# A fused delta-rule attention and mixture-of-experts kernel: the prologue's loads one place earlier, chunk 10's scores in the prologue, ten filler products instead of two

## The chip, the cores and the metric

One core of one Trainium2 chip runs the whole program. The metric is device time in microseconds (us) of one execution; a kernel's time is the median of its runs. The profile is of one further execution of the same program, and all times of single instructions are of that execution, counted from the start of its span.

## What is computed

The first half is a recurrence over 768 steps for 4 batches and 8 heads of width 48; its output, one row of 384 numbers per batch and step, goes through a two-level router into one of 16 experts.

```python
def _attn_ref(q, k, v, beta):
    k_n = k / (np.linalg.norm(k, axis=-1, keepdims=True) + 1e-06)
    state = np.zeros((B, H, D, D))
    for t in range(S):
        kt, vt, bt = (k_n[:, :, t], v[:, :, t], beta[:, :, t, None])
        y[:, :, t] = np.einsum('bhd,bhde->bhe', q[:, :, t], state)
        v_old = np.einsum('bhde,bhd->bhe', state, kt)
        state = state + bt[:, :, :, None] * np.einsum('bhd,bhe->bhde', kt, vt - v_old)
    return y

def _moe_ref(x, w_group, w_expert, w1, w2):
    ...
            h = np.maximum(xg[mask_e] @ w1[g, e], 0.0)
            ye = h @ w2[g, e]
            combined = g_w[mask_g][mask_e] * e_w[mask_e]
            out[tok_idx] = combined[:, None] * ye
```

The recurrence gives x of 3072 rows by 384; w1 is 384 by 1024 and w2 1024 by 384 for each expert. All data is 32-bit float.

## The kernel before

**Attention.** The 768 steps are cut into 24 chunks of 32 (NCH = 24), and four chunks make a group (RG = 4). A tile's 128 partitions are 4 batches by 32 steps. For each chunk `gram(u)` (L258 or L273) multiplies the keys with keys and queries on TensorE into PSUM, 32 products that the trace shows as 64 rows; ScalarE copies the two halves out, to `gt` (L278) and `gq` (L284). For each group `inverse(g)` works on VectorE for some 28 us in the prologue: a transpose (L313), a long row of multiply and add pairs (L382, L388), a transpose back into `mt` (L416). ScalarE spreads `mt` into `mtb` (L427), and VectorE makes one part of it (L425). `scale(u)` on VectorE (L463) multiplies the values of a chunk, which come with the tile `kv`, into `vh`.

`advance(u)` is one period of the recurrence, and each step in it needs the one before: products `a_ps` with the state (L486), ScalarE's copy `f` (L490), products `o_ps` with the state (L495), products `w_ps` with the inverse (L503), the copy `w` (L507), products into the state `s_ps` (L514), two copies to `s_bd` (L520), products that end `o_ps` (L528), the copy `x` (L537). Period 0 has no state yet, so it begins with `w_ps`. In each period stands one `gram` too, that of chunk u + LEAD (LEAD = 10), between `w_ps` and `s_ps`, and the three transposes `t_ps` (L554) and routing products `l_ps` (L456) of the chunk before.

**Loads.** Keys and queries of a chunk are one tile `kqt` of 448 KB, in a ring of NB = LEAD + 2 = 12 buffers; values are `kv`, 416 KB, in a ring of three; the constants come in two parts, of which the second (376.5 KB) holds the identity. All these loads are issued by SyncE's queue (SP) in program order.

**What sets the order in the prologue.** The order on every engine is the order of the code. Before period 0 there are twelve half or whole `gram` calls (chunks 0 to 3 keys only, 4 to 7 whole, then the query halves of 0 to 3), and behind them `gram(8)` and `gram(9)`. They write in turn to three places in PSUM, `g`, `begin0` and `begin1`; the last two lie where the state `s_ps` will lie, so the first writer of `s_ps` waits for ScalarE's copies out of them. A load is held back by `begin` (L800): ScalarE writes one column of the tile that the load will fill, and the load waits for that write. `bursts` says behind which `gram` ScalarE does so, and `after_gram` says it for `gram(8)` and `gram(9)`. Because ScalarE works in order, a load's gate opens when the copies of that `gram` are through. Behind `gram(9)` stand two products of the identity with constants (L834), 128 x 128 by 128 x 384, into `s_ps`; nothing reads their result, and the first product of the state overwrites it. Then `w_ps` of period 0 waits for `mtb`.

**Experts.** After the recurrence the rows are sorted by expert, and 16 experts follow one another on TensorE (L1113 and L1132). The change leaves this part alone.

Of the kernel before, what the change touches and what calls it, by code (L numbers as in the profile page):

```python
# [16 lines left out]
C = 32  # L17
RG = 4
SHARE = 0.61
LEAD = 10  # L20
FIXED, TILE = 1, 128
SLOTS = [224] * FIXED + [232, 220, 214, 208, 204, 202, 200, 198, 194, 190, 186, 184, 180, 174, 168]
ACT_STEP, PE_STEP, SOON, NEXT, TURN = "ScalarE", "TensorE", "end of the period", "next period", "its turn"
# [43 lines left out]
def deltanet_then_moe(  # L67
# [13 lines left out]
    nc = tc.nc  # L81
    B, H, S, D = shape
    NP = H // 2
    NCH = S // C
# [28 lines left out]
    wr = cp.tile([128, DC, NL], F32, name="wr")  # L113
# [64 lines left out]
    with ExitStack() as first:  # L178
# [10 lines left out]
        for n in range(2):  # L189
            homes.append(pse.tile([128, 2, 512], F32, tag=f"begin{n}", name=f"begin{n}"))  # L190
        NB, NV = LEAD + 2, 3
        LATE, SMALL, KR = NCH - LEAD, NGR - 1, 64 + D
        ENDING = NCH - 2
        halved = range(LATE, SMALL * RG)
        kqt_ = [ap_.tile([128, 2, NP, 128], F32, name=f"kqt{i}") for i in range(NB)]
        kv_ = [ap_.tile([128, NP * KR + H * D], F32, name=f"kv{i}") for i in range(NV)]

        def load_kq(u, a=None):
            half = slice(0, 2) if a is None else slice(a, a + 1)
            nc.sync.dma_start(out=kqt_[u % NB][0:KR, half],  # L200
                              in_=kq_d[u].rearrange("p (a j t) -> p a j t", a=2, j=NP)[:, half])

        def load_kv(u):
            nc.sync.dma_start(out=kv_[u % NV], in_=kv_d[u])
# [3 lines left out]
        def load_con(i):  # L208
            part = slice(cols[i], cols[i + 1])
            nc.sync.dma_start(out=con[:, part], in_=const_d[:, part])  # L210
# [13 lines left out]
        def of_kq(u, a=None):  # L224
            return (kqt_[u % NB][:, a or 0, 0], [lambda: load_kq(u, a)])

        bursts = {
            1: [of_kq(RG), of_kq(RG + 1)],
            RG: [of_kq(RG + 2), of_kq(RG + 3)],
            RG + 2: [of_kq(u, 1) for u in range(RG)]  # L230
                    + [(wr[:, 0], [lambda: nc.sync.dma_start(out=wr, in_=wr_d)])],
            2 * RG: [(kv_[0], [lambda: load_kv(0), lambda: load_con(1), lambda: load_kv(1)])],
            2 * RG + 2: [of_kq(2 * RG), of_kq(2 * RG + 1)],
        }
        after_gram = {2 * RG: [of_kq(2 * RG + 2), (kv_[2], [lambda: load_kv(2)])],
                      2 * RG + 1: [of_kq(2 * RG + 3), of_kq(NB)]}
        rooted = sm.tile([128, 1], F32, tag="rooted", name="rooted", bufs=1)
        gts, raws, gqs, mts, norm, vhs, xs, turned_over = {}, {}, {}, {}, {}, {}, {}, set()
        begun_with = {}
# [1 line left out]
        def gram(u, home=None, parts=(0, 1), paired=False):  # L241
# [39 lines left out]
            if 1 not in parts:  # L281
                return None
            raws[u] = wk.tile([128, H, C], F32, tag="gq", name=f"gq{u}", bufs=LEAD + 1)
            nc.scalar.activation(raws[u], g_out[:, :, 1, :], ACT.Copy)  # L284
# [471 lines left out]
        def start(task, share):  # L756
            behind.append(task)
            rate[task], due[task] = share, 0.0
# [24 lines left out]
        def allow(what):  # L783

            for task in list(behind):
                if held.get(task) is what:
                    push(task)
# [5 lines left out]
        with tc.manual_schedule(engines={mybir.EngineType.PE, mybir.EngineType.DVE,  # L793
# [3 lines left out]
            def begin(burst):  # L797

                for late, loads in burst:
                    nc.scalar.activation(late[:, 0:1], cut["tiny"], ACT.Copy)  # L800
                    for load in loads:
                        load()
# [19 lines left out]
                                  .to_broadcast([128, 4, 4, BL]))  # L822
            ahead = advance(0)
            next(ahead)
            for u in range(2 * RG, LEAD):
                gram(u, homes[u % len(homes)])
                begin(after_gram[u])
            begin_with.close()
# [1 line left out]
            s_ps = pst.tile([128, B, 512], F32, tag="state", name="s_ps")  # L830
            s_at = s_ps[:, :, 0:H * D].rearrange("p b (j d) -> p b j d", j=NP)
            sorted_in.update(at=s_ps[:, 0, H * D:H * D + T * 3 * NE], begun=True)
            for n in (H * D, H * D):
                nc.tensor.matmul(s_ps[:, 0, 0:n], lhsT=ident, rhs=con[:, cols[1]:cols[1] + n],  # L834
                                 start=True, stop=True, skip_group_check=True)
            second = inverse(1)
# [7 lines left out]
            while held.get(second) is not FACTOR:  # L844
                work(2)
            allow(FACTOR)
            ahead_of = {u: [u + LEAD] if u + LEAD < NCH else [] for u in range(NCH + 1)}
            begun, x_in = set(), {}

            def add_rows(j, **how):  # L850
# [12 lines left out]
            def only_first(u):  # L863

                nc.scalar.activation(kept[u], kept[u], ACT.Copy, scale=hots[:, u, 0:1])
# [29 lines left out]
            for u in range(NCH + 1):  # L895
                step = advance(u) if u < NCH else iter([None] * 4)
                turned = logits(u - 1) if u else iter([None] * 2)
                if 0 < u < NCH - 1:
                    mask(u + 1)
                if u == 2:  # L900
                    scale(RG)
                if u:
                    next(step)
                else:
                    step = ahead
                allow(FACTOR)
                allow(NEXT)
                allow(TURN)
                if u:
                    if u % RG == 0:  # L910
                        allow(READY)
                    allow(SPREAD)
                r = group_of.get(u - 2)
                if r is not None and group_of.get(u - 1) != r and r < EARLY:
                    start(route(r), 0.25)
                if u == NCH:
                    add_gathered(gathered, [0], range(2))
                later, ending = LATE <= u < NCH - 2, u + 2 == NCH
                if not later:
                    next(turned)  # L920
                if u == NCH:
                    only_first(near[1])
                if u:
                    allow(SPREAD)
                work(10)
                if u + 2 < NCH and u + 2 != RG:
                    scale(u + 2)
                if u < NCH and not later and not ending:
                    allow(SORT)
                if u == NCH:  # L930
                    add_gathered(gathered, [0], range(2, DC))
                    add_gathered(gathered, [1], range(DC - 1))
                next(step)
                if later:
                    next(turned)
                if u + 1 < NCH:
                    put_values(u + 1)
                if later:
                    for _ in range(1 + (u == NCH - 3)):
                        allow(SORT)  # L940
                if ending:
                    while SORT in held.values():
                        allow(SORT)
                    found_0 = read_found()
                    gathered = gather_first(found_0)
                for v in ahead_of[u]:
                    gram(v)
                if ahead_of[u] or later or ending:
                    next(step)
                    next(turned)  # L950
                else:
                    next(turned)
                if u >= NCH - 1:
                    allow(PE_STEP)
                    allow(ACT_STEP)
                if NCH - 2 <= u < NCH:
                    allow(SORT)
                work(9)
                if not ahead_of[u] and not later and not ending:
                    next(step)  # L960
                next(step)
                if u < NCH - 1:
                    allow(PE_STEP)
                    allow(ACT_STEP)
                if u == NCH - 1:
                    only_first(near[0])
                if u == 0:
                    for _ in range(2):
                        allow(SPREAD)
                work(14)  # L970
                allow(ACT_STEP)
                if u % RG == RG - 1:
                    allow(READY)
                allow(ROOTS)
                for r in range(EARLY, len(groups)):
                    if u == sum(groups[r]) + (r < BIG):
                        start(route(r), 0.4 if r < BIG else 0.6 if r == BIG else 1)
                allow(SOON)
                if u % RG == RG - 3 and u // RG + 2 < NGR:
                    start(inverse(u // RG + 2), SHARE)  # L980
                work(12)
                if u == 0:
                    mask(1)
                if 0 < u < NCH - NB:
                    load_kq(u + NB)
                if u < NCH - NV:
                    load_kv(u + NV)
                if u == NCH - 2:
                    x_in[0] = pst.tile([128, B, 512], F32, tag="state", name="x_ps")
                if u < NCH:  # L990
                    nc.sync.dma_start(out=x_dram[1 + u * 128:1 + (u + 1) * 128], in_=xs[u])
                if pieces and u + NB >= NCH:
                    pieces.pop(0)()
# [354 lines left out]
```

## Time and profile before

| what | number |
|---|---|
| median of 3 runs | 488.47 us (485.83 to 488.65) |
| the profiled execution: its own time | 488.77 us |
| its span in the trace, first to last instruction | 486.8 us |
| PE (products) busy | 444.6 us, 91% |
| DVE (VectorE) busy | 240.3 us, 49% |
| ACT (ScalarE) busy | 193.4 us, 40% |
| first `w_ps` of period 0 begins | 39.17 us |
| `w_ps` of period 1 begins | 49.21 us |
| last copy `x` of the recurrence begins | 207.57 us |

The span is 2.0 us shorter than the execution's own time; what lies around it is the same for both kernels, so that a difference in the span is taken as a difference in the time. In a row of the timeline the first number is the start in us, the second the time from the first to the last instruction of the row, then engine, line, operation, output<-inputs, shape and count, and in brackets how long the engine had been idle and what ended that. PEld is the load of a product's stationary operand, SPq the queue that issues loads. In a row of the stretches the columns are busy us (count of instructions) of PE, PEld, DVE, ACT and POOL, then the granted clock of TensorE, the busy share of the 16 DMA engines and GB/s.

### The profile page before, as it was taken

To read this page: it belongs to the slowest core of one execution; us is meant where nothing else is said; L and a number is where in the kernel's file an instruction comes from. 1 tells how busy PE (TensorE), PEld (TensorE's weight loads), DVE (VectorE), ACT (ScalarE), POOL (GpSimd) and SP (SyncE) were. 2 spreads that over 40 slices of the span, in tenths; PEclk is the share of its full clock that TensorE was granted. 3 is DMA by queue.
4 is the path that set the end of the run, shared out by engine and by line. 5 is a ranking of instruction groups with operands and counts; after the bars stand their busy time and mean duration, and the time that the engine had idled before them with its cause. 6 is when DMAs were issued, how large, how long until landed. Compare 5 with 4: busy or idle time off the path is not lost.

```text
span 486.8 us, 17982 instructions
## 1 busy us (share of the span) xinstructions
PE 444.6 (91%) x7670; PEld 421.8 (87%) x7670; DVE 240.3 (49%) x872; ACT 193.4 (40%) x413; POOL 182.7 (38%) x300
## 2 busy tenths in 40 slices
PE   3438989999999999999999999999999999999992
PEld 2336878888888888889999999999999999999992
DVE  4989989999999998473101220221122011201110
ACT  3336978898888866532112111111111111111110
POOL 0031340436327200104455445645645366256131
PEclk9998999999999999999999999999999999999998
DMA  5476454544344553308968867968896789678830
GB/s 164 144 194 202 152 159 147 158 148 145 105 146 146 155 159 100 96 20 225 368 219 242 293 216 225 314 208 274 277 313 219 254 307 332 231 221 280 289 103 26
DMA packets 56756, 97.05 MB, mean 199 GB/s; under 512 B 18974, under 2 KB 41433, under 8 KB 56675
## 3 DMA queue, kind: packets, MB, share of 16 engines
q1 hardware_dynamic: 50755, 85.89, 55.5%
q0 software_dynamic: 5920, 10.00, 6.7%
q8 instruction: 61, 1.00, 0.9%
q14 instruction: 20, 0.16, 0.1%
HBM read 81.75 MB, written 14.27 MB: 197 GB/s over the span
## 4 chain that ended last, share of the span: by engine, by line
PE 43%; DMA 19%; DVE 14%; issue 11%; ACT 6%; POOL 5%; SPq 1%; POOLq 0%; DVEq 0%; ACTq 0%
PE y_ps L1132 13%; PE h_ps L1113 13%; DMA out_dram<-yo,to_i 11%; DMA kqt<-in_kq_dram 5%; POOL xq L1085 4%; DVE m L388 4%; PE o_ps L528 3%; DVE below L382 3%; PE a_ps L486 2%; PE l_ps L456 2%; PE w_ps L503 2%; PE s_ps L514 2%; DMA y_dram<-yq 1%; PE o_ps L495 1%; ACT mtb L427 1%
## 5 line engine op out<-in xcount | busy, mean ns | idle before, releaser
L1132 PE MATMUL y_ps<-hid,w 128*128 128x224 f32 (+15 forms) x768 | 132.2, 331 | 0.0
L1132 PEld LDWEIGHTS y_ps<-hid,w 128*128 128x128 f32 x768 | 129.0, 190 | 0.3
L1113 PE MATMUL h_ps<-xt,w 128*128 128x232 f32 (+14 forms) x720 | 122.7, 330 | 0.0
L1113 PEld LDWEIGHTS h_ps<-xt,w 128*128 128x128 f32 x720 | 120.1, 190 | 0.3
L1085 POOL DMA_INDIRECT xq<-x_dram,from_q x92 | 87.6, 952 | 35.8 <-issue 23.7
L1135 DVE COPY yt<-y_ps 128x232 f32<-128x232 f32 (+13 forms) x14 | 5.1, 366 | 140.8 <-PE y_ps L1132 140.8
L1116 ACT ACTIVATE hid<-h_ps 128x448 f32<-128x448 f32 (+15 forms) x64 | 32.1, 502 | 100.2 <-PE h_ps L1113 100.2
L1144 POOL DMA_INDIRECT out_dram<-yo,to_i x32 | 34.1, 1065 | 92.5 <-DVE yo L1182 81.4
L1137 ACT ACTIVATE yt<-y_ps 128x224 f32<-128x224 f32 (+15 forms) x34 | 11.5, 337 | 116.6 <-PE y_ps L1132 116.6
L382 DVE TENSOR_TENSOR below<-m 128x16 f32<-128x16 f32 (+4 forms) x180 | 54.0, 306 | 0.2
L388 DVE TENSOR_TENSOR m<-m,below 128x16 f32<-128x16 f32 (+4 forms) x180 | 52.8, 294 | 0.4
L520 ACT ACTIVATE s_bd<-s_ps 48x768 f32<-48x768 f32 x46 | 37.0, 805 | 7.1 <-PE s_ps L514 6.6
L1182 DVE TENSOR_SCALAR yo<-yr,gate 128x384 f32<-128x384 f32 (+14 forms) x28 | 11.3, 421 | 43.1 <-DMA yr<-y_dram 35.5
L427 ACT ACTIVATE mtb<-mt,con 128x256 f32<-128x256 f32 x39 | 28.0, 742 | 0.0
L503 PEld LDWEIGHTS w_ps<-f,mtb 64*64 64x64 f32 x736 | 23.3, 134 | 5.4 <-ACT f L490 3.6
L503 PE MATMUL w_ps<-f,mtb 64*64 64x48 f32 x736 | 26.1, 220 | 1.3 <-ACT f L490 1.1
L514 PE MATMUL s_ps<-w,kv 32*112 32x96 f32 x736 | 24.8, 267 | 1.0 <-issue 0.4
L514 PEld LDWEIGHTS s_ps<-w,kv 32*112 32x112 f32 x736 | 20.7, 172 | 3.6 <-issue 0.8
L528 PE MATMUL o_ps<-w,gqm 64*64 64x48 f32 x576 | 21.4, 222 | 2.2 <-issue 2.1
L273 PE MATMUL g_ps<-kqt 48*32 48x64 f32 (+1 forms) x1152 | 16.7, 236 | 6.7 <-DMA kqt<-in_kq_dram 5.1
L388 DVE TENSOR_TENSOR m<-m,corner 128x28 f32<-128x28 f32 (+6 forms) x84 | 21.8, 260 | 0.0
L486 PE MATMUL a_ps<-s_bd,kqt 112*32 112x96 f32 x736 | 20.9, 254 | 0.9 <-ACT s_bd L520 0.8
(184 smaller groups left out, 547.6 us busy)
## 6 DMA issues: line engine op xcount, KB each, us to landing
w<-in_w_dram SPq DMA_DIRECT2D x29, 1536.0 KB, 10.6
kv<-in_kv_dram SPq DMA_DIRECT2D x24, 416.0 KB, 3.2
kqt<-in_kq_dram SPq DMA_DIRECT2D x20, 448.0 KB, 5.1
x_dram<-x SPq DMA_DIRECT2D x24, 192.0 KB, 2.8
w<-in_w_dram SPq DMA_DIRECT2D x24, 128.0 KB, 3.5
y_dram<-yq SPq DMA_DIRECT2D x36, 84.0 KB, 8.4
yr<-y_dram SPq DMA_DIRECT2D x14, 192.0 KB, 2.4
kqt<-in_kq_dram SPq DMA_DIRECT2D x8, 224.0 KB, 3.0
```

Source lines behind the costliest of these rows:

```text
L382: nc.vector.tensor_tensor(t, column.to_broadcast(like), row.to_broadcast(like), op=ALU.mult)
L388: nc.vector.tensor_tensor(to, to, t, op=ALU.add)
L427: nc.scalar.activation(mtb[:, rows, a], from_, ACT.Copy, scale=by)
L503: nc.tensor.matmul(w_ps[b, h], lhsT=mt[b, uu * H + (h % 2) * NP + h // 2], rhs=f[b, h], start=(h == 0), stop=True, skip_group_check=True)
L514: nc.tensor.matmul(s_at[0:KR, b, j], lhsT=k[quads[b], j, 0:KR], rhs=w[quads[b], 2 * j:2 * j + 2], start=(u == 0 and j == 0), stop=True, sk ...
L520: nc.scalar.activation(s_bd[rows, :, :, hh, :], s_at[rows, :, :, hh * D:(hh + 1) * D], ACT.Copy)
L528: nc.tensor.matmul(o_ps[b, h], lhsT=gq[b, hq].rearrange("p a t -> p (a t)"), rhs=w[b, h], start=(u == 0 and h == 0), stop=True, skip_group ...
L1085: nc.gpsimd.indirect_dma_start(out=xq[:, g, :], out_offset=None, in_=x_dram[:, :].rearrange("n (q c) -> (n q) c", q=4), in_offset=bass.Ind ...
L1113: nc.tensor.matmul(h_ps[:, k], lhsT=w1[:, j, (f + k) * 128:(f + k + 1) * 128], rhs=xt[:, j, 0:R], start=(j == 0), stop=(j == DC - 1), skip ...
L1116: nc.scalar.activation(hid[:, f:f + 2], h_ps, ACT.Relu)
L1132: nc.tensor.matmul(y_ps, lhsT=w2[:, f, j * 128:(j + 1) * 128], rhs=hid[:, f], start=(f == 0), stop=(f == FC - 1))
L1144: put = nc.gpsimd.indirect_dma_start(out=out[:, :], out_offset=bass.IndirectOffsetOnAxis(ap=to[0:P, i:i + 1], axis=0), in_=yo[0:P, :], in_ ...
```

## The change

Four edits, all before or in period 0:

- Every entry of `bursts` moves up: chunks 4 to 7 are all let go behind the second `gram` call instead of two of them two calls later; the query halves of chunks 0 to 3 and the routing weights `wr` behind call 4 instead of 6; `kv` 0, the second constants and `kv` 1 behind call 6 instead of 8; chunks 8 and 9 behind call 8 instead of 10; chunk 10 and `kv` 2 behind call 10 instead of `gram(8)`; chunk 11 behind `gram(8)` instead of `gram(9)`.
- Chunk 12 has no gate any more: its load stands at the end of period 0, like those of the later chunks. SP's order of loads stays what it was.
- `gram(10)` moves from period 0 into the prologue, behind `gram(9)`; period 0 then holds no `gram`.
- The products of constants in front of `w_ps` become ten instead of two.

```diff
-LEAD = 10
+LEAD, IDLE = 10, 10
...
         bursts = {
-            1: [of_kq(RG), of_kq(RG + 1)],
-            RG: [of_kq(RG + 2), of_kq(RG + 3)],
-            RG + 2: [of_kq(u, 1) for u in range(RG)]
-                    + [(wr[:, 0], [lambda: nc.sync.dma_start(out=wr, in_=wr_d)])],
-            2 * RG: [(kv_[0], [lambda: load_kv(0), lambda: load_con(1), lambda: load_kv(1)])],
-            2 * RG + 2: [of_kq(2 * RG), of_kq(2 * RG + 1)],
+            1: [of_kq(u) for u in range(RG, 2 * RG)],
+            RG: [of_kq(u, 1) for u in range(RG)]
+                + [(wr[:, 0], [lambda: nc.sync.dma_start(out=wr, in_=wr_d)])],
+            RG + 2: [(kv_[0], [lambda: load_kv(0), lambda: load_con(1), lambda: load_kv(1)])],
+            2 * RG: [of_kq(2 * RG), of_kq(2 * RG + 1)],
+            2 * RG + 2: [of_kq(2 * RG + 2), (kv_[2], [lambda: load_kv(2)])],
         }
-        after_gram = {2 * RG: [of_kq(2 * RG + 2), (kv_[2], [lambda: load_kv(2)])],
-                      2 * RG + 1: [of_kq(2 * RG + 3), of_kq(NB)]}
+        after_gram = {2 * RG: [of_kq(2 * RG + 3)], 2 * RG + 1: (), LEAD: ()}
...
-            for u in range(2 * RG, LEAD):
+            for u in range(2 * RG, LEAD + 1):
                 gram(u, homes[u % len(homes)])
                 begin(after_gram[u])
...
-            for n in (H * D, H * D):
+            for n in IDLE * (H * D,):
                 nc.tensor.matmul(s_ps[:, 0, 0:n], lhsT=ident, rhs=con[:, cols[1]:cols[1] + n],
                                  start=True, stop=True, skip_group_check=True)
...
-            ahead_of = {u: [u + LEAD] if u + LEAD < NCH else [] for u in range(NCH + 1)}
+            ahead_of = {u: [u + LEAD] if u and u + LEAD < NCH else [] for u in range(NCH + 1)}
...
-                if ahead_of[u] or later or ending:
+                if ahead_of[u] or not u or later or ending:
                     next(step)
                     next(turned)
...
-                if 0 < u < NCH - NB:
+                if u < NCH - NB:
                     load_kq(u + NB)
```

On ScalarE, in the middle of the prologue, the order before is this. `kqt_105` to `kqt_108` are the buffers of chunks 0 to 3, `kqt_109` to `kqt_112` those of 4 to 7, `kqt_113` to `kqt_116` those of 8 to 11; `kv_117` and `kv_119` are those of `kv` 0 and 2; a row of 128x1 is a gate.

```order
L278 ACTIVATE gt_258<-begin_103 128x8x32
L284 ACTIVATE gq_412<-begin_103 128x256
L284 ACTIVATE gq_446<-begin_104 128x256
L800 ACTIVATE kv_117<-con 128x1
L284 ACTIVATE gq_485<-g_ps_452 128x256
L284 ACTIVATE gq_519<-begin_103 128x256
L800 ACTIVATE kqt_113<-con 128x1
L800 ACTIVATE kqt_114<-con 128x1
L284 ACTIVATE gq_557<-begin_104 128x256
```

The same stretch with the change:

```order
L799 ACTIVATE kv_117<-con 128x1
L277 ACTIVATE gt_262<-begin_103 128x8x32
L283 ACTIVATE gq_416<-begin_103 128x256
L283 ACTIVATE gq_450<-begin_104 128x256
L799 ACTIVATE kqt_113<-con 128x1
L799 ACTIVATE kqt_114<-con 128x1
L283 ACTIVATE gq_489<-g_ps_456 128x256
L283 ACTIVATE gq_523<-begin_103 128x256
L799 ACTIVATE kqt_115<-con 128x1
L799 ACTIVATE kv_119<-con 128x1
L283 ACTIVATE gq_561<-begin_104 128x256
```

Each gate has moved up by one step of the table, past two `gram` calls and their copies.

On TensorE, around the beginning of period 0, the order before is this (`gram(8)`, `gram(9)`, two products, then the period):

```order
L273 MATMUL begin_104<-kqt_113 32x64 x32
L273 MATMUL g_ps_734<-kqt_114 32x64 x32
L834 MATMUL s_ps<-con 128x384 x2
L503 MATMUL w_ps_855<-vh_688,mtb_827 64x48 x16
L273 MATMUL g_ps_876<-kqt_115 32x64 x32
L514 MATMUL s_ps<-w_872,kv_117 112x96 x16
L528 MATMUL o_ps_693<-w_872,gqm_830 64x48 x16
```

With the change:

```order
L272 MATMUL begin_104<-kqt_113 32x64 x32
L272 MATMUL g_ps_736<-kqt_114 32x64 x32
L272 MATMUL begin_103<-kqt_115 32x64 x32
L833 MATMUL s_ps<-con 128x384 x10
L502 MATMUL w_ps_896<-vh_692,mtb_868 64x48 x16
L513 MATMUL s_ps<-w_913,kv_117 112x96 x16
L527 MATMUL o_ps_697<-w_913,gqm_871 64x48 x16
```

The 32 products of chunk 10 have moved ahead of `w_ps`, and ten products of constants stand where two stood; `s_ps` now follows `w_ps` directly.

More of the change, by code (lines that the diff above doesn't have):

```diff
@@ L958, in deltanet_then_moe @@
                 work(9)
-                if not ahead_of[u] and not later and not ending:
+                if u and not ahead_of[u] and not later and not ending:
                     next(step)
```

## Prediction

> **What bounds the kernel now.** I read three views in this order: the chain of waits for the first 90 us, then the timeline there by engine, then stretches for the clock, the DMA and VectorE. The change touches only the first 50 us; from the second period on everything keeps its order, so the question is when period 0 begins and how long it lasts. The chain of waits, start and length in us:
>
> ```profile
> 25.79 1.79 issue
> ...
> 28.79 5.92 DMA kqt<-in_kq_dram
> ...
> 34.84 1.19 PE begin L273 x61
> 36.12 0.64 ACT gt L278
> 36.75 0.21 ACT gq L284
> 37.07 3.94 DMA kqt<-in_kq_dram
> ...
> 41.15 0.85 PE g_ps L273 x49
> 42.00 0.97 PE s_ps L514 x32
> 42.97 0.71 PE o_ps L528 x20
> 43.68 1.58 issue
> 45.27 0.88 PE o_ps L528 x12
> ```
>
> By this chain the prologue is bound by loads that are issued late: chunk 8 is issued at 28.79 and arrives 5.92 later, its copies open the gate of chunk 10 at 37.07, that arrives 3.94 later, and chunk 10's products in period 0 hold up `s_ps`. But a chain shows one line of descent. The timeline shows a second one, VectorE's inverse, that ends at almost the same time:
>
> ```profile
> 28.77 0.56 DVE L463 TENSOR_TENSOR vh<-kv,normt 128x384 f32<-128x384 f32 x1 [1.36 <-DMA kv<-in_kv_dram]
> 35.61 1.25 DVE L416 STREAM_TRANSPOSE mt<-m 128x1024 f32<-128x1024 f32 x1
> 37.02 2.21 PE L834 MATMUL s_ps<-con 128*128 128x384 f32 x4
> 38.05 0.72 ACT L427 ACTIVATE mtb<-mt,con 128x256 f32<-128x256 f32 x1
> 39.17 1.14 PE L503 MATMUL w_ps<-vh,mtb 64*64 64x48 f32 x32
> 40.35 0.49 ACT L507 ACTIVATE w<-w_ps 128x384 f32<-128x384 f32 x1 [1.57 <-PE w_ps L503]
> 42.23 0.56 DVE L463 TENSOR_TENSOR vh<-kv,normt 128x384 f32<-128x384 f32 x1 [0.75 <-DMA kv<-in_kv_dram]
> ```
>
> `mt` is ready at 36.86, ScalarE is still copying late scores and makes `mtb` only from 38.05 to 38.77, and the two products of constants end at 39.2. So `w_ps` of period 0, at 39.17, has two last waits at once, and both come from the late chunks 8 and 9. I call its start W.
>
> **Loads earlier, and VectorE.** The stall of 1.36 for `kv` 0 at 28.77 and that of 0.75 for `kv` 2 at 42.23 go, since both loads leave their gates two scores earlier. VectorE does the same work in the same order, so `mt` comes at 36.86 - 1.36 = 35.5 and `mtb`, with 0.72 on ScalarE and the first product some 0.1 behind it, allows W = 36.3. That is the floor. What is left is when PE is free.
>
> **When chunk 10 arrives.** All these loads stand in one queue whose order stays, so I count bytes. The first row is SP issuing chunks 4 to 7, the second the first two being used; the other two are stretches in which the queue was full.
>
> ```profile
> 7.15 7.85 SPq L200 DMA_DIRECT2D kqt<-in_kq_dram  x4
> 12.05 2.20 PE L273 MATMUL begin<-kqt 48*32 48x64 f32 x128 [3.89 <-DVE r L349]
> 31.00:32.00 1.00, 0.00 (x0) 0.00 (x0) 1.00 (x4) 0.00 (x0) 0.77 (x2) 1.00 1.01 265
> 41.00:42.00 1.00, 0.85 (x68) 0.79 (x68) 0.48 (x4) 0.36 (x1) 0.00 (x0) 1.00 1.03 325
> ```
>
> Up to the end of chunk 10 the queue carries four chunks, four halves, `wr`, `kv` 0, the constants, `kv` 1 and three chunks: 7 x 448 + 4 x 224 + 30 + 2 x 416 + 376.5 = 5270 KB or 5.40 MB. From 8.2, about 1 us after the first issue, at 290 GB/s (between 265 and 325) that takes 18.6 us; the halves' gate stands behind the copies of chunk 4, which are through only when the first four chunks are nearly in, so I add a pause of 0.9; and two chunks of 0.92 MB, issued at 7.15, were both in use only at some 13.1, so of their 5.9 us some 1.6 lie behind the data. Chunk 10 is there at 8.2 + 18.6 + 0.9 + 1.6 = 29.3; with a little for the constants' smaller packets I take 30.0, between 27.3 (at 325) and 31.1 (at 265). Chunks 8 and 9 come before it and cost nothing more.
>
> Then its products, 1.19 like those of the chain at 34.84, and its two copies before PSUM is free for `s_ps`, 1.0 as between the end of those at 36.03 and the row at 37.02: the products of constants begin at 30.0 + 1.2 + 1.0 = 32.2.
>
> **Ten products of constants.** Before, two of them are four rows in 2.21 us, 0.55 each, and they begin on a slow clock. The pace of such rows in the long run is that of the experts:
>
> ```profile
> L1132 PE MATMUL y_ps<-hid,w 128*128 128x224 f32 (+15 forms) x768 | 132.2, 331 | 0.0
> ```
>
> The line's own answer has the shortest, median and longest of the four in ns:
>
> ```profile
> L834 PE MATMUL s_ps<-con x4: 486/626/1007, 37.0 to 38.8; 128*128 128x384 f32 x4
> ```
>
> 132.2 / 768 = 0.172 us for 224 columns, so 384 columns take 0.295. Ten products are twenty rows: 5.9 us at full clock, 11.8 at half. The first four at the measured 2.21 and sixteen at 0.295 make 6.9; because PE idles for 1.0 us before them here, where before it came straight from two dense scores, I take 7.5. So PE is free at 32.2 + 7.5 = 39.7, and W = 39.7, which is 0.5 **later** than before. Its bounds are 36.3 (the floor) and, with chunk 10 at 31.1 and half clock throughout, 33.3 + 11.8 = 45.1. All that the loads win before W is eaten by eight more products.
>
> **Period 0.** What comes back is behind W. Rows of ScalarE and of PE in period 0, and of an ordinary start of `s_ps` in period 2:
>
> ```profile
> 43.03 1.62 ACT L520 ACTIVATE s_bd<-s_ps 48x768 f32<-48x768 f32 x2 [0.15 <-PE s_ps L514]
> 46.19 0.49 ACT L537 ACTIVATE x<-o_ps 128x384 f32<-128x384 f32 x1 [1.54 <-PE o_ps L528]
> 46.58 1.36 ACT L427 ACTIVATE mtb<-mt,con 128x256 f32<-128x256 f32 x2
> 47.85 0.47 ACT L490 ACTIVATE f<-a_ps 128x384 f32<-128x384 f32 x1
> 48.22 0.74 ACT L427 ACTIVATE mtb<-mt,con 128x256 f32<-128x256 f32 x1
> 49.32 0.49 ACT L560 ACTIVATE xt<-t_ps 128x384 f32<-128x384 f32 x1 [0.35 <-PE t_ps L554]
> 49.71 0.74 ACT L427 ACTIVATE mtb<-mt,con 128x256 f32<-128x256 f32 x1
> 50.40 0.49 ACT L507 ACTIVATE w<-w_ps 128x384 f32<-128x384 f32 x1
> ...
> 57.17 0.49 ACT L507 ACTIVATE w<-w_ps 128x384 f32<-128x384 f32 x1
> 57.85 1.04 PE L514 MATMUL s_ps<-w,kv 32*112 32x96 f32 x32
> ```
>
> Before, from W to the copy `w` of period 1: 50.40 - 39.17 = 11.2. With the change: `w` is copied by W + 1.7 (40.35 + 0.49 - 39.17), `s_ps` begins 0.2 later as in period 2 and takes 1.04, to W + 2.9; from there ScalarE is the bound, with 1.62 + 0.49 + 1.36 + 0.47 + 0.74 + 0.49 + 0.74 = 5.9 and 0.1 of hand-over, so `w` of period 1 is copied at W + 8.9. That is 2.3 less. It holds the wait for chunk 10 and its products (1.0), and most of the 1.58 of "issue"; the slow `a_ps` and `o_ps` behind it hide under ScalarE.
>
> The 1.58 is open. I read it, like the 1.79 at 25.79, as the next piece of PE's program not being there: between the two stalls lie 381 rows of PE (101 of the query halves, 2 x 64, 4, 32, 64, 32 and 20) and as many weight loads, 762 instructions, three pieces of 254, and the page's queue of instructions moved 61 pieces in 1.00 MB. Sixteen more rows of products move that border from row 20 of `o_ps` to row 4. There it can cost nothing (ten slow products give 7.5 us to fetch it) up to 1.5: with the same 3.3 from the start of `s_ps` to the resumption, `o_ps` ends at W + 6.1 where the copies to `s_bd` end at W + 4.6. I take 0.2, nearer to nothing.
>
> [...]
>
> **The rest.** Chunk 12 is let go when the gate of chunk 11 is, and is used only in period 2. `kv` 3 stands behind it on SP and waits for `s_ps` of period 0 as before. In the periods after, VectorE is the engine with the least room:
>
> ```profile
> 155.00:162.00 7.00, 6.11 (x227) 5.48 (x219) 7.00 (x34) 6.39 (x12) 5.98 (x9) 1.00 0.45 151
> 157.62 0.55 DVE L463 TENSOR_TENSOR vh<-kv,normt 128x384 f32<-128x384 f32 x1
> 158.72 0.49 ACT L473 ACTIVATE a_ps<-vh 128x384 f32<-128x384 f32 x1
> ```
>
> It is full there (7.00 of 7.00), and the values of chunk 17 end at 158.17, 0.55 before ScalarE takes them. VectorE itself comes 1.36 + 0.75 = 2.1 earlier, so a lead of up to 2.65 passes through to the experts; more would be lost there.
>
> **The sum.** Later W +0.5, period 0 -2.3, the border +0.2: **-1.6 us**. The profiled execution of 488.77 becomes 487.2; it lay 0.3 above the median of the runs shown, so the median goes from 488.47 to **486.9**. One per cent, about what a measurement of this kernel can tell from no change, is 4.9 us; this lies well inside it.
>
> **Rivals.** *A, the products end early.* The loads come at 325 GB/s and the products run on full clock from the start: 27.3 + 2.2 + 5.9 = 35.4, W at the floor of 36.3, 2.9 earlier; with period 0 that is 5.2, of which VectorE lets 2.65 through: 485.8. For it speaks that chunks 8, 9 and 10 precede the products closely; against it the four rows of L834, which began slow behind two scores.
>
> *B, nothing is left.* The border costs its 1.5 and the clock falls in period 0 again. Rows of before, slow products and the same ones one period later, and a stretch with the granted clock at half:
>
> ```profile
> 46.08 1.51 PE L486 MATMUL a_ps<-s_bd,kqt 112*32 112x96 f32 x32
> 54.06 0.87 PE L486 MATMUL a_ps<-s_bd,kqt 112*32 112x96 f32 x32
> 46.00:47.00 1.00, 1.00 (x28) 0.93 (x28) 1.00 (x7) 0.81 (x2) 0.00 (x0) 0.50 0.09 30
> ```
>
> The row loses 0.64, and I let 0.6 reach ScalarE's copies. With +0.5, -2.3, +1.5 and +0.6 the sum is +0.3: 488.8. I think the fall came from the idle 1.58 before it, which then goes with it; a clock that falls for another reason would stay. [...]
>
> *C, slower: the products hold `w_ps` back.* They stay on the slow clock, 11.8 us from 32.2, and W becomes 44.0, 4.8 later; less 2.3 and with 0.2 that is +2.7: 491.2. It decides from the point where the products last over 9.1 us or begin later than 33.8. For it: they wait for the very last score and stand in PE's order before `w_ps`, while `mtb` waits idle from 36.3. Against: before, the shortest of four rows already took 0.49 where the longest took 1.01.
>
> **Chances.** The forecast, up to 1.4 to either side (485.5 to 488.3), 0.55; A 0.15; B 0.15; C 0.15. The range reaches down past A's 485.8 by 0.9, since the runs shown scatter over 2.8, and up past B to 489.6: 484.9 to 489.6. Outside it lie C's price and what is worse, and the far end of A, together no more than 0.2. Faster by over 1% needs more than A gives, 0.04; slower by over 1% needs C at its bound, 0.02; within 1%, 0.94.
>
> **What would show it.** In the changed profile: no wait for `kv` 0 or `kv` 2 on VectorE; `mt` near 35.5; chunk 10's products near 30; twenty rows of L833 over 6 to 9 us that end last before `w_ps`, with `mtb` done some 3 us earlier; W near 39.7; from W to `w` of period 1 about 9 us; no half clock in period 0. If W comes before 37.5 or after 42, or if period 0 is not 2 us shorter, the sum is wrong; if the lead at period 1 is there and the end is not earlier, VectorE or a new "issue" stall took it back.

## The result and the profile after

| | before | after |
|---|---|---|
| median, us | 488.06 (485.83 to 489.18, 6 runs) | 494.08 (493.50 to 500.48, 6 runs) |
| ratio of after to before | | 1.0136, 95% interval 1.0086 to 1.0185 |
| span of the profiled execution | 486.8 | 492.5 |
| W, start of the first `w_ps` | 39.17 | 45.69 |
| copy `w` of period 0 | 40.35 | 46.87 |
| copy `w` of period 1 | 50.40 | 53.87 |
| copy `w` of period 16 | 157.87 | 161.17 |
| copy `w` of period 17 | 163.92 | 169.80 |
| last copy `w` | 205.33 | 210.59 |

The kernel is slower by 1.4% in the ratio; the two medians alone are 1.2% apart. The table is a ledger that is read downwards: W comes 6.5 us later, period 0 (from copy `w` to copy `w`) is 3.05 shorter, the next fifteen periods keep what is left (3.3), period 16 is 2.6 longer, and the end is 5.3 later in the recurrence and 5.7 over the span.

The chain of waits of the changed kernel up to period 0 (start, length, what):

```profile
22.54 5.21 DMA kqt<-in_kq_dram
27.89 0.66 PE begin L272 x26
28.55 2.09 issue
30.63 0.84 PE begin L272 x37
31.51 0.80 PE g_ps L272 x57
32.36 0.38 PE begin L272 x24
32.74 2.00 issue
34.74 0.90 PE begin L272 x38
35.67 0.61 ACT gt L277
...
36.55 9.21 PE s_ps L833 x20
45.76 1.09 PE w_ps L502 x32
```

Before, two waits for loads, 5.92 and 3.94, filled this place. Now one stands at its head. Two pieces named "issue", 4.09 us together, and one block of products, 9.21, have taken over: TensorE is ready, its data is there, and its program is not; that this is what "issue" means here is shown in the part on why the prediction was wrong. The timeline of TensorE has the other "issue" stalls of the prologue, and between them stand 127 or 128 rows each time (36 + 64 + 27 from the second to the third):

```profile
17.05 0.74 PE L272 MATMUL g_ps<-kqt 48*32 48x64 f32 x34 [1.55 <-issue]
...
21.39 0.61 PE L272 MATMUL begin<-kqt 48*32 48x32 f32 x36 [2.40 <-issue]
21.79 0.88 PE L272 MATMUL g_ps<-kqt 48*32 48x32 f32 x64
22.45 0.49 PE L272 MATMUL begin<-kqt 48*32 48x32 f32 x27
25.74 1.32 PE L272 MATMUL begin<-kqt 48*32 48x32 f32 x101 [2.80 <-issue]
...
30.63 0.85 PE L272 MATMUL begin<-kqt 48*32 48x64 f32 x37 [2.09 <-issue]
...
34.74 0.89 PE L272 MATMUL begin<-kqt 48*32 48x64 f32 x38 [2.00 <-issue]
```

Work resumes at 17.05, 21.39, 25.74, 30.63 and 34.74, that is every 4.1 to 4.9 us. The stall before 25.74 also holds back a load. In the timeline, ScalarE's copy of those products opens chunk 10's gate, and SP issues the load behind it:

```profile
26.44 0.39 ACT L283 ACTIVATE gq<-begin 128x256 f32<-128x256 f32 x1 [3.35 <-PE begin L272]
...
26.72 0.19 ACT L799 ACTIVATE kqt<-con 128x1 f32<-128x1 f32 x1
...
26.94 0.31 SPq L200 DMA_DIRECT2D kqt<-in_kq_dram  x1
```

Then rows around `w_ps`, picked from the timeline of all engines:

```profile
33.43 1.25 DVE L415 STREAM_TRANSPOSE mt<-m 128x1024 f32<-128x1024 f32 x1
36.38 0.73 ACT L426 ACTIVATE mtb<-mt,con 128x256 f32<-128x256 f32 x1
36.55 9.21 PE L833 MATMUL s_ps<-con 128*128 128x384 f32 x20 [0.92 <-ACT gq L283]
45.69 1.14 PE L502 MATMUL w_ps<-vh,mtb 64*64 64x48 f32 x32
46.87 0.49 ACT L506 ACTIVATE w<-w_ps 128x384 f32<-128x384 f32 x1 [9.76 <-PE w_ps L502]
46.87 0.56 DVE L462 TENSOR_TENSOR vh<-kv,normt 128x384 f32<-128x384 f32 x1 [7.87 <-PE w_ps L502]
```

`mtb` is ready at 37.11; for 8.6 us the only thing in front of `w_ps` is the products of constants. And VectorE stands still for 7.87 us: `vh` has two buffers, the values of chunk 2 go where those of chunk 0 lie, and the first `w_ps` still has to read these. Its row begins at 46.87, against 42.23 before.

### The profile page after: what moved, and what is told of

It is laid out like the page before. It is cut to its first block, busy times and chain, and to the rows that moved or that the text cites. A ratio compares the mean times of both kernels' runs of the same rounds, so it can differ in the third digit from the quotient of the medians.

```text
span 492.5 us, 18012 instructions
## 1 busy us (share of the span) xinstructions
PE 451.5 (92%) x7686; PEld 425.7 (86%) x7686; DVE 240.2 (49%) x872; ACT 192.8 (39%) x412; POOL 183.2 (37%) x300
## 4 chain that ended last, share of the span: by engine, by line
PE 56%; DVE 16%; DMA 14%; ACT 5%; issue 5%; POOL 2%; SPq 1%; DVEq 0%; POOLq 0%; ACTq 0%
PE y_ps L1131 19%; PE h_ps L1112 19%; DMA out_dram<-yo,to_i 5%; DVE m L387 4%; DVE below L381 4%; DMA y_dram<-yq 3%; DMA kqt<-in_kq_dram 3%; PE s_ps L513 2%; PE w_ps L502 2%; DMA yr<-y_dram 2%; PE s_ps L833 2%; PE o_ps L527 2%; PE a_ps L485 2%; ACT s_bd L519 2%; PE l_ps L455 1%
## 5 line engine op out<-in xcount | busy, mean ns | idle before, releaser
L1181 DVE TENSOR_SCALAR yo<-yr,gate 128x384 f32<-128x384 f32 (+14 forms) x28 | 11.2, 418 | 41.7 <-DMA yr<-y_dram 34.9
L317 POOL MEMSET m<- 128x256 f32 (+4 forms) x30 | 4.1, 190 | 55.5 <-DVE m L312 55.5
L272 PE MATMUL begin<-kqt 48*32 48x64 f32 (+1 forms) x576 | 10.3, 280 | 14.8 <-issue 9.3
L272 PEld LDWEIGHTS begin<-kqt 48*32 48x32 f32 x576 | 8.4, 145 | 16.0 <-issue 15.0
```

## The experiments

The theory: the loss is made in front of W, by the ten products and by chunk 10's scores, whose rows stand behind the program's stalls; the earlier loads by themselves are a small gain. The rival: the loss is VectorE's wait of 7.87, which the later periods pay. A second rival is the half clock in a later period. Ratios are against runs of the kernel before on the same chip (median 491.96 beside the first four experiments, 492.61 beside the last four); the row of the change is that of the result. W, period 0 and the span are of one profiled execution, which can lie some us from the median of its kernel: that of before_idle10 took 492.06 where the median is 496.43, that of idle2 490.30 where it is 493.77.

| kernel | loads | chunk 10's scores | products | W | period 0 | span | ratio (95%) |
|---|---|---|---|---|---|---|---|
| before | old | period 0 | 2 | 39.17 | 10.05 | 486.8 | 1 |
| after | new | prologue | 10 | 45.69 | 7.00 | 492.5 | 1.0136 (1.0086 to 1.0185) |
| before_idle10 | old | period 0 | 10 | 43.51 | 7.15 | 490.2 | 1.0101 (1.0066 to 1.0136) |
| idle2 | new | prologue | 2 | 40.14 | 7.02 | 488.4 | 1.0041 (1.0011 to 1.0070) |
| loads_only | new | period 0 | 2 | 37.09 | 7.19 | 485.0 | 0.9952 (0.9915 to 0.9990) |
| scores_only | old | prologue | 2 | 45.86 | 8.66 | 495.2 | 1.0085 (1.0042 to 1.0128) |
| loads_one | new | period 0 | 1 | 36.54 | 8.96 | 490.6 | 0.9957 (0.9913 to 1.0001) |

Period 0 is from its copy `w` to that of period 1.

**idle2: the change with two products of constants instead of ten.**

```diff
-LEAD, IDLE = 10, 10
+LEAD, IDLE = 10, 2
```

> The change with two products of constants instead of ten. Products theory (the loss is the time of the ten products between the last copies at 36.5 and w_ps): two products take some 2.2 us, w_ps of period 0 begins near 38.7 instead of 45.7, period 0 keeps its 7.0 us, no wait of 7.9 us on VectorE; 3 to 4 us faster than before, near 484.5. Rival (earlier loads are worth nothing, since TensorE then waits for its program instead): w_ps no earlier than 40 or period 0 longer again, 487 to 490.

Measured: 493.77 us, ratio 1.0041 (1.0011 to 1.0070). TensorE's timeline:

```profile
35.48 0.89 PE L272 MATMUL begin<-kqt 48*32 48x64 f32 x38 [2.00 <-issue]
37.28 2.93 PE L833 MATMUL s_ps<-con 128*128 128x384 f32 x4 [0.91 <-ACT gq L283]
40.14 1.78 PE L502 MATMUL w_ps<-vh,mtb 64*64 64x48 f32 x32
```

The theory on record, W near 38.7 and 3 to 4 us gained, missed; W came where the rival had it, no earlier than 40. The products still begin at 37.28, since the same stall of 2.00 splits chunk 10's scores in front of them. Taking eight away brings W from 45.69 to 40.14 and takes off about 0.9% (1.0136 to 1.0041); it does not make the change a gain. Period 0 is as short as with ten (7.02).

**before_idle10: the kernel before with ten products, nothing else.**

```diff
-            for n in (H * D, H * D):
+            for n in 10 * (H * D,):
```

> The kernel before with ten products of constants, nothing else changed. Products theory: they begin at 37.0 as before and take 7 to 9 us, w_ps begins at 44 to 46, VectorE waits for it at the values of chunk 2; the chunk-10 products of period 0 no longer wait for their load and the clock is up, so period 0 is some 8 us; 490 to 494, slower than before. Rival (the loss is in the loads and the moved scores): within 1 us of before.

Measured: 496.43 us, ratio 1.0101 (1.0066 to 1.0136). TensorE's timeline:

```profile
35.45 8.13 PE L834 MATMUL s_ps<-con 128*128 128x384 f32 x20
43.51 1.13 PE L503 MATMUL w_ps<-vh,mtb 64*64 64x48 f32 x32
```

W is 4.3 later (a little less than the 44 to 46 on record) and period 0 2.9 shorter, although chunk 10's scores still stand in it. So the length of period 0 before, 10.05, was not the price of these scores: with W at 43.5 chunk 10's load has arrived and the stall of the program has passed, and 7.15 is left. Eight products cost 1% by themselves, about as much as removing them from the change takes off. The profile has only 1.4 us of this at the beginning of period 1 (51.84 against 50.40); where the rest is lost isn't shown.

**loads_only: the new places of the loads; chunk 10's scores and two products as before.**

```diff
-            for u in range(2 * RG, LEAD + 1):
+            for u in range(2 * RG, LEAD):
...
-            ahead_of = {u: [u + LEAD] if u and u + LEAD < NCH else [] for u in range(NCH + 1)}
+            ahead_of = {u: [u + LEAD] if u + LEAD < NCH else [] for u in range(NCH + 1)}
```

(with LEAD, IDLE = 10, 2 and the two conditions in the period as before)

> The change's loads alone: two products, and the scores of chunk 10 back in period 0. Products theory: w_ps is bound by the inverse, which is ready at 34.7 with these loads, so it begins near 36; period 0 holds the chunk-10 products again and perhaps a stall of 2 us for the program, 8 to 10 us; 484 to 486. Rival (earlier loads are worth nothing): w_ps after 38, 488.

Measured: 489.43 us, ratio 0.9952 (0.9915 to 0.9990), the only kernel here whose whole interval lies below 1. TensorE's timeline:

```profile
27.91 1.32 PE L272 MATMUL begin<-kqt 48*32 48x32 f32 x101 [4.72 <-issue]
...
32.35 0.85 PE L272 MATMUL begin<-kqt 48*32 48x64 f32 x37 [1.98 <-issue]
...
34.23 2.93 PE L833 MATMUL s_ps<-con 128*128 128x384 f32 x4 [0.16 <-ACT gq L283]
37.09 1.19 PE L502 MATMUL w_ps<-vh,mtb 64*64 64x48 f32 x32
```

W is 2.1 earlier than before (37.09, where 36 was expected) and period 0 takes 7.19 (8 to 10 were expected), so period 1 begins 4.9 earlier (45.53 against 50.40). At the end of the span 1.8 of it is left. From 46 us to 170 TensorE waits 5.4 us for "issue" here, against 2.2 in the kernel before, about what was lost; VectorE is nearly full in both (99% and 98% from 45 to 170), so which of the two takes it back isn't shown. Against idle2 the difference is the scores' place alone: 0.9952 and 1.0041, W 37.09 and 40.14, period 0 7.19 and 7.02. The move of the scores pays 3 us to win 0.2.

**vh3: the change with a third buffer for the scaled values.**

```diff
-            vh = wk.tile([128, H, D], F32, tag="vh", name=f"vh{u}")
+            vh = wk.tile([128, H, D], F32, tag="vh", name=f"vh{u}", bufs=3)
```

> The change as it is, with three buffers instead of two for the scaled values, so that those of chunk 2 need not wait until w_ps of period 0 has read those of chunk 0. If that wait of 7.9 us on VectorE is what costs the 2.6 us in period 16: w_ps still at 45.7, VectorE not idle in front of it, the lag behind before stays near 3.3 us from period 4 to the end, 491.5. If the 2.6 us have another cause (the clock, the router's work): 494 as the change.

Measured: 496.68 us, ratio 1.0096 (1.0064 to 1.0129), W 46.08. The waits of VectorE show that the run didn't answer its question:

```profile
DVE vh L462 <- DMA kv<-in_kv_dram: 4.7, 1, 4.7
```

One place further on VectorE waits for the values of chunk 3, whose load needs the third buffer of `kv` and so period 0's `s_ps`. Most of the wait has only changed its name. Even so period 16 takes 6.05 here, and the period whose `o_ps` at 123.11 and `a_ps` at 124.84 are slow (1.80 and 1.51 against 1.13 and 0.87) takes 9.40: the long period goes with the slow rows and not with VectorE's wait.

**free_dve: the same, with a fourth buffer for `kv`, loaded in the prologue.**

```diff
-        NB, NV = LEAD + 2, 3
+        NB, NV = LEAD + 2, 4
...
-            2 * RG + 2: [of_kq(2 * RG + 2), (kv_[2], [lambda: load_kv(2)])],
+            2 * RG + 2: [of_kq(2 * RG + 2), (kv_[2], [lambda: load_kv(2), lambda: load_kv(3)])],
```

(and the third buffer of `vh`)

> The changed kernel with a third buffer for the scaled values and a fourth one for the keys and values, whose load then goes out in the prologue: VectorE waits neither for the first w_ps nor for chunk 3's keys and values. Theory 1 (the ten products and the stalls before them are the loss; VectorE has time to catch up): w_ps still starts at 45.5 to 46.5 us and the time stays 1.009 to 1.014 of before. Rival (the wait of VectorE, 7.87 us, comes back as the long period 16): the same start, but no period of over 8 us that begins with a late copy of the values by ScalarE, and a time of 1.004 to 1.008.

Measured: 497.73 us, ratio 1.0107 (1.0068 to 1.0146). Timeline of TensorE and VectorE:

```profile
47.48 1.13 PE L502 MATMUL w_ps<-vh,mtb 64*64 64x48 f32 x32
48.66 0.56 DVE L462 TENSOR_TENSOR vh<-kv,normt 128x384 f32<-128x384 f32 x1 [0.53 <-PE w_ps L502]
```

VectorE's wait has shrunk from 7.87 to 0.53, and the loss is still 1.1%. W is later than foreseen, 47.48, because one stall of the program took 3.10 here. Period 16 takes 6.06 and not 8.63; but period 7 takes 9.31, with the granted clock at half from 103.8 to 107.2 us. So VectorE's wait is not the loss, which lies in front of W; and what made period 16 long fits the half clock, which in this run fell elsewhere.

**scores_only: the kernel before with chunk 10's scores in the prologue, nothing else.**

```diff
-                      2 * RG + 1: [of_kq(2 * RG + 3), of_kq(NB)]}
+                      2 * RG + 1: [of_kq(2 * RG + 3)], LEAD: [of_kq(NB)]}
...
-            for u in range(2 * RG, LEAD):
+            for u in range(2 * RG, LEAD + 1):
...
-            ahead_of = {u: [u + LEAD] if u + LEAD < NCH else [] for u in range(NCH + 1)}
+            ahead_of = {u: [u + LEAD] if u and u + LEAD < NCH else [] for u in range(NCH + 1)}
```

(and the two conditions in the period; the gate of chunk 12 moves behind the scores of chunk 10)

> The kernel before with one part of the change: the scores of chunk 10 stand in the prologue, two products of constants as before, the loads in their old order. Theory 1 (what stands in front of the first state products costs what it makes them wait for): chunk 10's load, which landed at about 40.3 us in the kernel before, now gates the products and so the first w_ps, whose start moves from 39.17 to 43 to 45 us; period 0 falls from 10.05 to about 7.0 us, so period 1 begins at 50.5 to 52 us against 50.40, and the time is 1.000 to 1.005 of before. Rival (the move is worth what period 0 loses, and costs its own 0.85 us of products): w_ps at about 40 us, period 1 at about 47.5, ratio 0.994 to 0.996.

Measured: 496.58 us, ratio 1.0085 (1.0042 to 1.0128). TensorE's timeline:

```profile
40.91 1.19 PE L273 MATMUL begin<-kqt 48*32 48x64 f32 x64 [3.80 <-DMA kqt<-in_kq_dram]
43.00 2.93 PE L834 MATMUL s_ps<-con 128*128 128x384 f32 x4 [0.90 <-ACT gq L284]
45.86 1.95 PE L503 MATMUL w_ps<-vh,mtb 64*64 64x48 f32 x32
52.02 1.51 PE L486 MATMUL a_ps<-s_bd,kqt 112*32 112x96 f32 x32
```

Theory 1 was right that the load now holds up W, and too low in size: W is 45.86 where 43 to 45 was expected, and period 0 takes 8.66 instead of 7.0. TensorE had idled 3.80 us before these rows, and the rows `w_ps` and `a_ps` (1.95 and 1.51, against 1.14 and 0.87 elsewhere) run at half pace into period 0. The rival, which credits the move with what period 0 loses, is ruled out.

**loads_one: loads_only with one product of constants.**

```diff
-LEAD, IDLE = 10, 2
+LEAD, IDLE = 10, 1
```

> As loads_only (the loads of the change alone), but with one product of constants in front of w_ps instead of two. Theory 1 (what stands in front of w_ps costs its length until VectorE's part is what comes last): the one product ends about 35.7 us, the part of VectorE and ScalarE about 36.5, w_ps starts at 36.4 to 36.8 against 37.09 and the time is 0.993 to 0.996 of before. Rival (the products earn their time by keeping the clock up): w_ps and period 0 run at a lower clock, 1 us or more longer in all, 0.997 to 1.001.

Measured: 490.59 us, ratio 0.9957 (0.9913 to 1.0001). TensorE's timeline:

```profile
32.84 1.65 PE L833 MATMUL s_ps<-con 128*128 128x384 f32 x2
36.54 1.95 PE L502 MATMUL w_ps<-vh,mtb 64*64 64x48 f32 x32 [2.05 <-ACT mtb L426]
...
43.16 1.51 PE L485 MATMUL a_ps<-s_bd,kqt 112*32 112x96 f32 x32
```

Both theories hold, each for its part. W is 36.54 and VectorE's and ScalarE's `mtb` comes last, as theory 1 says. But TensorE idles 2.05 us for it, and then period 0 is slow up to its `o_ps` at 44.44 (1.46 against 0.84 a period later; `w_ps` 1.95 against 1.19 in loads_only) and takes 8.96 against 7.19. In these two executions period 0 ran at full pace behind two products and not behind one. In the time one and two products can't be told apart.

**rows_more: loads_only with 64 more rows at 6 us.**

```diff
-                for j in range(NP):
+                for j in 3 * list(range(NP)) if u else range(NP):
                     for b in pairs:
```

> As loads_only, but the scores of chunk 1's first half are computed three times over into the same place, which puts 64 more rows on TensorE's list at about 6 us, where it idles until 11 us. Theory 1 (the program itself arrives in blocks of about 128 such rows, and the long stalls marked as issue are TensorE waiting for its next block): each such stall stands 64 rows earlier in the work: the first one splits the scores of chunk 5 (29 rows, then the rest) where it split those of chunk 6, and the one in front of 32.35 us stands in the second halves of chunks 0 to 3; TensorE then has up to 64 more rows to do behind the last stall, 0.8 us, and w_ps starts at 37 to 38.5 us against 37.09. Rival (the stalls belong to these products, to their loads, copies or banks): they stay in front of the same rows, split 29 rows into chunk 6 and 26 rows into chunk 8, and w_ps stays at 37.1. Time 0.993 to 1.002 of before by either.

Measured: 493.22 us, ratio 1.0038 (0.9993 to 1.0083). TensorE's timeline:

```profile
14.95 0.68 PE L272 MATMUL begin<-kqt 48*32 48x64 f32 x30 [0.57 <-DMA kqt<-in_kq_dram]
19.45 0.74 PE L272 MATMUL begin<-kqt 48*32 48x64 f32 x33 [3.82 <-issue]
...
32.47 0.66 PE L272 MATMUL begin<-kqt 48*32 48x32 f32 x37 [1.98 <-issue]
...
37.15 0.89 PE L272 MATMUL g_ps<-kqt 48*32 48x64 f32 x38 [1.98 <-issue]
37.97 2.71 PE L833 MATMUL s_ps<-con 128*128 128x384 f32 x4
40.61 1.14 PE L502 MATMUL w_ps<-vh,mtb 64*64 64x48 f32 x32
```

On the place theory 1 was right to within a row: the first long stall, 3.82, splits chunk 5 behind 30 rows, the one before 32.47 stands in the second half of a chunk, and the rival's places are empty. The stalls belong to the count of rows in the program, not to these products or their loads. On the size both were wrong: W is 40.61, 3.5 later than in loads_only, where at most 1.4 was allowed for, and the ratio lies above the 1.002 on record. I had overlooked that one more border of the program then falls in front of `w_ps`: in chunk 9, 26 rows from its beginning, with 1.98 of its own.

## Why the prediction was wrong

**The step that failed is W, on record as +0.5 and measured as +6.5.** It had two parts.

*When the products begin: 32.2 on record, 36.55 measured.* The prediction counted the bytes in the queue and had chunk 10 there at 30.0. But the load was not issued until 26.94, because its gate waits for ScalarE's copy of products that stood behind a stall of 2.80, and by the trace's record it landed at 31.8. It was not alone in being late: TensorE, which had stood for 2.09 within the rows of chunk 8, was through with chunk 9 only at 32.0 and went on to chunk 10's rows without a wait for the load, as the chain shows. Either would have cost nearly 2 us. Then came 2.00 more in the middle of its 64 rows. In the prediction the two "issue" rows of before were read correctly as the program arriving in pieces, but were applied to one border between two pieces only, that in period 0 (+0.2). The rows are the same ones in both kernels, and so are the borders: before, several of them passed unseen while TensorE waited for loads. Bring the loads forward, and the program is what comes last. That the borders move with the number of rows is shown by rows_more. That the stalls are a fetch of the program is shown by the trace's records of the transfers on queue q8, packets of 16 KB named "instruction" (us):

| packet begins | packet ends | TensorE resumes |
|---|---|---|
| 14.53 | 15.64 | 17.05 |
| 18.63 | 19.86 | 21.39 |
| 23.44 | 24.47 | 25.74 |
| 28.04 | 29.14 | 30.63 |
| 32.17 | 33.27 | 34.74 |

Each stall ends 1.3 to 1.5 us behind a packet, and each next packet sets out only 1.5 to 2.3 us after TensorE has resumed. The trace of the kernel before has the same: packets end at 26.32 and 43.88, and TensorE resumes at 27.59 and 45.27. Why a packet does not set out sooner, and whether the loads in the queue hold it back, was not tried. The row of the page on the queue of instructions (packets, MB, share of the DMA engines) fits it: it moved 62 packets of 16 KB, and the page counts 7686 rows of products and as many weight loads on TensorE, 15372 together or 248 for a packet, where 127 or 128 rows with their weight loads are 254 or 256:

```profile
q8 instruction: 62, 1.02, 0.8%
```

In the changed prologue the five stalls of the table cost 10.8 us of TensorE's idle time (1.55 + 2.40 + 2.80 + 2.09 + 2.00).

*How long they last: 7.5 on record, 9.21 measured.* The weight loads of these products show the pace:

```profile
37.35 0.34 PEld L833 LDWEIGHTS s_ps<-con 128*128 128x128 f32 x1 [0.30 <-issue]
37.99 0.34 PEld L833 LDWEIGHTS s_ps<-con 128*128 128x128 f32 x1 [0.30 <-issue]
...
41.19 0.34 PEld L833 LDWEIGHTS s_ps<-con 128*128 128x128 f32 x1 [0.30 <-issue]
41.72 3.42 PEld L833 LDWEIGHTS s_ps<-con 128*128 128x128 f32 x11 [0.20 <-issue]
```

0.64 us from row to row up to 41.7, about 0.32 from there. The slow stretch lasts 5.2 us or eight rows, not the four that the prediction had. In the kernel before, where dense scores stood directly in front, the first record of the full clock comes 1.4 us after the products begin (38.4 and 37.02), here 5.1 (41.6 and 36.55); that the idle 2.00 and 0.92 in front of them, with 38 rows between, is the reason is a reading. The fast rows were too cheap as well: the prediction took 132.2 / 768 for the price of 224 columns, but that group mixes sixteen widths from 168 to 232, 199 in the mean. That the products hold `w_ps` back is the mechanism of rival C, and the point from which it decides was given as 9.1 us or a start after 33.8: both are passed. C's own price, W = 44.0, came from half clock throughout and a start at 32.2; the start was the larger part of the miss (4.35 against 1.7).

**Period 0 was nearly right.** On record -2.3, measured -3.05: from W to the copy `w` of period 1 8.18 instead of 8.9. ScalarE is the bound there, as forecast, but its copies overlap at their ends: 5.35 from the first `s_bd` (48.52) to `w` (53.87), where the prediction added their lengths to 5.9. But before_idle10 shows that it was not the moved scores that made it shorter.

**The border in period 0** (+0.2 on record) cost nothing: the 32 rows of `o_ps` run in one piece (48.38, 1.14). By the count the border lies some five rows into them now; there were ten products' time to bring the next block, and its packet ran from 36.68 to 37.81.

**VectorE's step was wrong.** It was to come 2.1 earlier, through the earlier values. `mt` did come early (34.68, even before the 35.5 on record), but the second buffer of `vh` ties VectorE to W, and it came 4.64 later. The prediction named who reads `vh` and not who has to have read it before it is written again. By free_dve this costs nothing that a measurement can tell; it is a wrong step without a price here.

**The half clock.** It has gone from period 0, as forecast, and stands in period 16. A stretch of the changed kernel, and two rows of its timeline there:

```profile
165.00:166.00 1.00, 1.00 (x53) 0.99 (x55) 1.00 (x6) 0.96 (x2) 1.00 (x2) 0.50 0.79 203
```

```profile
165.01 1.50 PE L532 MATMUL o_ps<-w,gqm 32*32 32x48 f32 x64
166.44 1.51 PE L485 MATMUL a_ps<-s_bd,kqt 112*32 112x96 f32 x32
```

From 164.5 to 167.9 the clock is at half and period 16 takes 8.63 instead of 6.05. I ascribed the dip to the idle 1.58 in period 0; with that gone, the dip was only elsewhere. In the profiles it stands at 45 us (before), 165 (after), 83 (idle2), 100 (before_idle10), 123 (vh3, by its slow rows), 104 (free_dve), 134 (scores_only), and in loads_only, loads_one and rows_more there is none in the recurrence. So the 2.6 of period 16, out of 5.7 us between the two profiles, go with such a dip, while the one of before cost its share inside the 10.05; no run changed the dip alone. Which kernel gets one, and where, stays open.

**The sum**, with what the parts measured: W +6.5, period 0 -3.05, period 16 +2.6, the rest -0.4: 5.7 in the span, and 5.6 between the two profiled executions (494.40 - 488.77).

The version that the experiments point to is loads_only: the new places for the loads, and neither of the other two edits. Against the kernel before it is faster by half a per cent (0.1 to 0.85% by its interval), and the changed kernel lies 1.4% on the other side.

## What to carry to other kernels

Before pulling loads forward, look at the small "issue" stalls of the engine that waits for them: if they recur after the same number of instructions, the program itself comes at a rate (in this prologue 127 or 128 rows in 4.1 to 4.9 us), and here a load that was ahead of it won nothing more: chunk 10's landed at 31.8 and TensorE came to its rows only at 32.0. Work moved into this prologue was paid in front of the first step of the recurrence (chunk 10's scores took W from 37.09 in loads_only to 40.14 in idle2), while the place it leaves may have been long for other reasons; the test is to change one of the two alone. Filler products were not free here: two put W 0.55 us later than one, ten put it 4.3 later than two (before_idle10), and with one most of period 0 ran at half pace, though the time of the kernel did not show that.

## What the runs showed of the hardware

In the changed prologue 127 or 128 rows of products with their weight loads stood between two of TensorE's waits for its program. In the first 38 us such a wait cost between 0.5 us (0.53 in rows_more) and 4.7 us (4.72 in loads_only), and the waits of the table above and the two of the kernel before ended 1.3 to 1.5 us behind the end of an instruction packet on queue q8.

The products of constants of the changed kernel ran at half pace for 5.2 us (0.64 a row against 0.32), although the stretches of the profile give the granted clock as 1.00 there. The trace's first record of the clock stands only at 41.6 (38.4 in the kernel before), so that the column says nothing of the time before it, and the rows are to be trusted. The later changes of the clock in the changed kernel stand at 164.49, to 0.50, and at 167.91, back to 1.00; in the kernel before at 45.20 and 48.62. Each of these two dips lasts 3.41 us. In front of the one at 164.49 TensorE's idle stretches were 1.00 us (before 159.99) and 1.06 us (before 162.66). What sets off a dip was not shown.
